# Where an odd chunk's stored factors are loaded: behind the even chunk's last tables, or at the odd chunk's turn

## The chip, the cores and the metric

The kernel runs on one core of a Trainium2 chip. The metric is the device time of one execution in microseconds; a comparison uses the median of several runs. The core has five engines that matter here, each with an instruction order of its own: TensorE (PE, matrix products), VectorE (DVE, elementwise work), ScalarE (ACT, exponentials, sines), GpSimd (POOL, here only an issuer of DMAs) and SyncE (SP, the main issuer of DMAs). An instruction at the head of an engine's order that waits for something holds up all behind it on that engine.

## The reference

Two independent computations on a sequence of 2048 with 576 channels stand side by side in the output. The first is a long convolution whose kernel K comes from a diagonal state space:

```python
P = jnp.exp(logdA[:, :, None] * l[None, None, :])
K = jnp.einsum("dn,dnl,dn->dl", Cc, P, dB).real
...
Kf = rfft2(K padded to 2L)
Uf = rfft2(u padded to 2L)
y = irfft2(Uf * Kf)[..., :L] + u * Dskip
```

The second is multi-query attention with 32 heads of 18 channels that share one key and one value head:

```python
q = (x @ wq).reshape(B, S, H, Dh)
k = x @ wk
v = x @ wv
p = softmax(einsum("bhqd,bkd->bhqk", q, k) * Dh ** -0.5)
o = einsum("bhqk,bkd->bhqd", p, v).reshape(B, S, H * Dh) @ wo
```

Everything is in float32.

## The kernel before

**Attention is the frame.** It runs over four query chunks of 512 rows, eight groups of four heads, sixteen blocks of 128 keys and two pairs of heads: 1024 score tiles, two to a step, so 512 steps. Each round of three tiles issues the scores on PE (L520), the exponentials on ACT (L531) and, some tiles later, the products with the values (L829). Beside this PE has filler work: the query projections (`q`), the output projections (`op`) and the whole convolution.

**The convolution runs in 12 chunks of 48 channels**, each in two halves that are generators:

- `front(k)` makes the kernel K of chunk k. `factors(k)` prepares three tiles of factors, `f`, `r` and `m` (128 x 1248 each, 624 KB), and the small `w`. Two half chunks follow, each with `tables(k, s)` on DVE, which multiplies the factors out into `tab`, and `kgen(k, s, ksb)` on PE, which contracts the tables into a PSUM bank that DVE copies to `ksb`. At the end `ksb` goes through DRAM (`kd`, L1234) into another layout (`kt`, L1236).
- `back(k)` transforms the input (`us`, from the matmuls hu and lu) and the kernel (`ks`, from hk and lk), multiplies the spectra (`pt`, `acc`) and transforms back (`iy`).

**Even and odd chunks differ in `factors`.** The factors need exponentials and sines from ACT, which interrupt the softmax and change ACT's table. So the even chunk k computes them for k and for k + 1 together, with the second set in one tile `two`, and stores `two` in DRAM (`parked`, L1146, shown as `park<-two`). The odd chunk k + 1 loads `f`, `r`, `m` and `w` from there (L1106) and begins with `r * m` and `f * m`. `f`, `r`, `m` and `w` have one buffer each, shared by all chunks, as do `sum` (which shares the buffer of `m`) and `tab`.

**The order of the engines.** PE, ACT, DVE and POOL run in the order in which the program issues their instructions; SP is not named there, so the framework may set the order of its DMAs by what is ready:

```python
with tc.manual_schedule(engines={mybir.EngineType.PE, mybir.EngineType.Activation, mybir.EngineType.DVE, mybir.EngineType.Pool}):
```

The order of the four is made by a planner while the program is built. A `Clock` carries the modelled times of PE (`t`), DVE (`v`) and ACT (`a`). The generators yield a kind, a time from which they are ready, and whether they hold the one PSUM bank for fillers: "v" is DVE work, "p" PE work, "w" waits, "b" waits for a good place for the block of sines. `Stream.go` lets a stream advance when its time has come and, for PE work, when there is credit. `Conv.turn` starts the next turn, `back(k)` beside `front(k + 1)`, only when both halves of the turn before have ended. In `factors`, the odd chunk yields "v" with the time `K.t + 7.0` behind its loads, so that the planner doesn't order `r * m` sooner than 7 us after them.

The constants at the top tune the planner: how far DVE is ordered ahead of PE (AHEAD), how much credit fillers get and keep (LEAST, CAP, DEBT, MOST), how large a gap must be (GAP, GAP_NEW), when a product is put off (DEFER), when the projections are ahead or late (LEAD, SLOPE, LEFT, URGENT), and so on.

Of the kernel before, what the change touches and what calls it, by code (L numbers as in the profile page):

```python
# [9 lines left out]
F32 = mybir.dt.float32  # L10
# [7 lines left out]
P = 128  # L18
# [19 lines left out]
NP = 8  # L38


RATE = 6.983
PACE = 1.7672
AHEAD = 0.4952
TOTAL = 604.4861
LAST = 813.2825
DEFER = 0.378
NAUG = 5
LEFT = 1.1655
CAP = 1.5491
DEBT = 0.6604  # L50
GROUP = 0.1377
HOLD = 0.3071
LEAD = 1.8204
MOST = 0.4269
LEAST = 0.3048
NEAR = 1.3779
SLOPE = 0.851
SOON = 1.3672
URGENT = 8.8421
BACK = 2  # L60
HELD = 0
GAP = 0.2663
GAP_NEW = 0.3191

LATE = {1: [0], 3: [1], 5: [2], 6: [3]}

ND = 48
NCK = D // ND
NSB = 2
TB = ND // 4 // NSB  # L70
NE = 4 * ND
NF = 26
# [5 lines left out]
class Clock:  # L78
# [13 lines left out]
    def near(self):  # L92

        return NEAR if self.t + SOON > min(self.due, self.last) else 0.0

# [58 lines left out]
class Stream:  # L154
# [3 lines left out]

    def __init__(self, gen, clock, ahead=AHEAD):
        self.gen, self.k, self.ahead = gen, clock, ahead  # L160
# [44 lines left out]
class Attention:  # L205
# [294 lines left out]
    def fetch(self, group):  # L500

        while self.next < min(64, 2 * group + NAUG) and 2 * self.next + 2 <= self.queried:
            c, pr = divmod(self.next, 16)
            t = self.aug[self.next].bitcast(F32)
            qd, sd = self.qd[c]
            for j in range(2):
                h = 2 * pr + j
                self.nc.sync.dma_start(t[64 * j:64 * j + 54, :], qd[:, h * DH:h * DH + DH, :])
                self.nc.sync.dma_start(t[64 * j + 54:64 * j + 55, :], sd[h:h + 1, :])
            self.ready.add(self.next)  # L510
            self.next += 1
# [226 lines left out]
    def late(self):  # L738

        s = self.step  # L740
        if self.due < 128 and self.due - s < 2 * self.q_left + 14:
            return True
        return (84, 168, 252, 282)[s // 128] - self.units > LEFT * (128 * (s // 128) + (120, 120, 120, 116)[s // 128] - s)

# [17 lines left out]
    def main(self, conv, flag):  # L762
# [22 lines left out]
        def fill(then, wait=True):  # L785
# [3 lines left out]
            while more:  # L789
# [3 lines left out]
                late = self.late()  # L793
                ahead = self.units - LEAD * self.step
                for st in (prep, side, conv) if urgent else (prep, conv, side):
                    if st is side and side.kind == "p" and not (urgent or side.holds) and conv.lags(self.step):
                        continue
                    spare = credit - LEAST
                    if st is side and not (urgent or late or side.holds):
                        spare -= SLOPE * max(ahead, 0.0)  # L800
                    elif st is side and side.holds:
                        spare += HOLD
                    wait = then - K.t - (GAP_NEW if st is side and not urgent and not side.holds else GAP)
# [13 lines left out]
            state["filled"] += K.t - t  # L817
            state["credit"] = max(state["credit"] - (K.t - t), -DEBT)

        def product(h):  # L820
# [11 lines left out]
            state["credit"] -= 0.44  # L832
            self.k.last = K.t + GROUP if kb >= 14 else 1e9
            if f == 0:
# [9 lines left out]
        for r in range(0, len(pairs), NS):  # L844
# [31 lines left out]

            state["credit"] = min(state["credit"] + NS / 2 * (0.88 + min(max((TOTAL - state["filled"]) / max(LAST - s, 20), 0.45), MOST)), CAP + 0.88)

# [4 lines left out]
            while behind < target:  # L883
                fill(free() - 0.44 * (target - behind), False)

                if behind >= target - 2 and K.t + 0.44 > free() + DEFER:
                    break
# [110 lines left out]
class Conv:  # L998
# [57 lines left out]
    def arguments(self, k, w, f, r, m):  # L1056
# [32 lines left out]
        if k > 1:  # L1089
            self.load(k + 2)  # L1090

    def factors(self, k):

        nc, V, p1, K = self.nc, self.V, self.pf, self.k
        tt = V.tensor_tensor
        mu, ad, sb = ALU.mult, ALU.add, ALU.subtract
        shp = [P, ND, NF]
        ch = lambda t, n: t.unsqueeze(2).broadcast_to([P, ND, n])
        w = p1.tile([P, 3, ND], F32, tag="w", name=f"w{k}")
        f = p1.tile(shp, F32, tag="f", name=f"f{k}")  # L1100
        r = p1.tile(shp, F32, tag="r", name=f"r{k}")
        m = p1.tile(shp, F32, tag="sum", name=f"m{k}")
        if k % 2:
            n = ND * NF
            for j, t in enumerate((f, r, m, w)):
                nc.sync.dma_start(t, self.parked[:, j * n:min((j + 1) * n, 3 * n + 3 * ND)].rearrange("p (c n) -> p c n", n=t.shape[2]))  # L1106
            yield "v", K.t + 7.0, False
        else:
            two = p1.tile([P, 3 * ND * NF + 3 * ND], F32, tag="tab", name=f"two{k}")
            part = lambda j, n: two[:, j * ND * NF:j * ND * NF + n * ND].rearrange("p (c n) -> p c n", n=NF if n == NF else ND)  # L1110
            f2, r2, m2, w2 = part(0, NF), part(1, NF), part(2, NF), part(3, 3)
            def sines(cos, sin):
                nc.scalar.activation(sin, sin, AF.Sin, scale=TWO_PI)
                nc.scalar.activation(cos, cos, AF.Sin, scale=-TWO_PI, bias=self.hp)
            one, two_ = self.arguments(k, w, f, r, m), self.arguments(k + 1, w2, f2, r2, m2)
            if k == 0:
                take = lambda g, n: [next(g, None) for _ in range(n)]
                take(one, 2)
                take(two_, 1)
                take(one, 1)  # L1120
                take(two_, 1)
                yield "v", 0.0, False
                take(one, 9)
                sines(r, f)
                yield "v", 0.0, False
                take(two_, 3)
                yield "v", 0.0, False
                take(two_, 9)
                sines(r2, f2)
                nc.scalar.activation(self.one, self.one, AF.Exp)  # L1130
                yield "v", 0.0, False
                for j in (2, 3):
                    self.load(j)
            else:
                yield from one
                yield "v", 0.0, False
                yield from two_
                yield "v", K.v + 0.3, False
                nc.scalar.activation(m, m, AF.Exp)
                nc.scalar.activation(m2, m2, AF.Exp)  # L1140
                K.act(2.5)
                yield "b", K.v + 0.3, False
                sines(r, f)
                sines(r2, f2)
            self.parked = self.dr.tile([P, 3 * ND * NF + 3 * ND], F32, tag="park", name=f"park{k}")
            nc.sync.dma_start(self.parked, two)  # L1146
            yield "v", K.act(7.7 if k > 0 else 0.0) + 0.3, False
        tt(r, r, m, op=mu)
        yield "v", 0.0, False
        tt(f, f, m, op=mu)  # L1150
        yield "v", 0.0, False

        c8 = lambda t: t[:, :, 0:8]
        t1 = p1.tile([P, ND, 8], F32, tag="tmp", name=f"t1_{k}")
        t2 = p1.tile([P, ND, 8], F32, tag="dif", name=f"t2_{k}")
        tt(t2, c8(r), ch(w[:, 1, :], 8), op=mu)
        tt(t1, c8(f), ch(w[:, 1, :], 8), op=mu)
        yield "v", 0.0, False
        tt(c8(r), c8(r), ch(w[:, 0, :], 8), op=mu)
        tt(c8(f), c8(f), ch(w[:, 0, :], 8), op=mu)  # L1160
        yield "v", 0.0, False
        tt(c8(r), c8(r), t1, op=sb)
        tt(c8(f), c8(f), t2, op=ad)
        sm = p1.tile(shp, F32, tag="sum", name=f"sum{k}")
        df = p1.tile([P, ND, 10], F32, tag="dif", name=f"dif{k}")
        yield "v", 0.0, False
        tt(df, f[:, :, 16:], r[:, :, 16:], op=sb)
        yield "v", 0.0, False
        tt(sm, r, f, op=ad)
        yield "v", 0.0, False  # L1170
        self.fac = r, f, sm, df
# [50 lines left out]
    def front(self, k):  # L1222

        nc = self.nc
        yield from self.factors(k)
        ksb = self.pf.tile([P, 4, NSB, 16, TB], F32, tag="ksb", name=f"ksb{k}")
        for s in range(NSB):
            yield from self.tables(k, s)
            yield from self.kgen(k, s, ksb)
        while self.kt is not None:  # L1230
            yield "w", 0.0, False
        kt = self.p1.tile([P, 4, NSB, 16, TB], F32, tag="kt", name=f"kt{k}")
        kd = self.dr.tile([P, 4, NSB * 16 * TB], F32, tag="kd", name=f"kd{k}")
        nc.sync.dma_start(kd, ksb.rearrange("p h s c d -> p h (s c d)"))  # L1234
        for h in range(4):
            nc.sync.dma_start(kt[32 * h:32 * h + 32].rearrange("p g s c d -> p g (s c d)"), kd[:, h].rearrange("(g p) x -> p g x", p=32))  # L1236
        self.kt, self.kt_ready = kt, self.k.t + 9.0
# [151 lines left out]
    def go(self, step, credit, lock):  # L1389
        self.turn()  # L1390
        lag = step * RATE - self.work
        if lag < -20.0:
            return False
        ahead = AHEAD + min(max(lag, 0.0) / 20.0, 1.0)
        for st in self.streams:
# [16 lines left out]
    def lags(self, step):  # L1412
        return self.work < step * PACE and any(st.live and st.kind == "p" for st in self.streams)

# [120 lines left out]
```

## Time and profile before

| | |
|---|---|
| median of 3 runs | 1183.37 us (1183.21 to 1183.97) |
| the profiled execution, its own time | 1182.26 us |
| its span, first to last instruction | 1180.1 us |
| mean clock granted to TensorE | 0.994 of full speed |
| bytes moved by DMA | 132.06 MB, on average 112 GB/s |
| softmax exponentials on ACT (L531) | 992 of 1032 ns, 941.3 us |
| products with the values on PE (L829) | 529.7 us |
| scores on PE (L520) | 349.5 us |

Times in the profile are microseconds from the start of the span unless marked ns. A row of a timeline has the start, the duration, the engine, the line, the operation with its output and inputs by name, the shape, the count, and in brackets the idle time before it with what ended that. SPq rows are DMAs as SP issues them: their duration is that of the issue, not of the transfer. A row of a table of groups ends with busy time, mean ns of one, the idle time before the group and what ended it. In a row of the waits stand who waited, for whom, the total in us, how often, and the longest. Rows of the chain of work that ended last have a start, a duration and what worked. Matmul durations overlap on PE, so its busy time is that of the engine and not a sum of durations.

### The profile page before, as it was taken

Reading aid. Unit: us, or ns where it says so; the run is one execution under the profiler, and the core shown is the slowest. Engines: PE = TensorE matmul, PEld = TensorE weight load, DVE = VectorE, ACT = ScalarE, POOL = GpSimd, SP = SyncE. Lnnn points to the kernel's source line nnn. Section 1 sums busy time; section 2 is a strip of 40 time slices with the busy share of each in tenths; the row PEclk is TensorE's granted clock in tenths of the full one; section 3 lists DMA queues with packets and bytes.
Section 4 is the critical chain, followed back from the end, with each engine's and each line's share of the span. In section 5 each row is a group of like instructions: output and inputs, shape, how many; then the busy total and the mean of one; then the engine's idle time right before and its main releaser. Section 6 shows DMA issues by size and latency. Waiting matters only on the chain.

```text
span 1180.1 us, 41335 instructions
## 1 busy us (share of the span) xinstructions
PE 1132.4 (96%) x17962; PEld 601.1 (51%) x17962; DVE 959.8 (81%) x1703; ACT 1038.0 (88%) x1092; POOL 95.0 (8%) x151
## 2 busy tenths in 40 slices
PE   7999999899999999999989999988999999999997
PEld 2555555455555455555545555544544545555553
DVE  7858979886997965996988698679799797799575
ACT  5899889889989988888998988888999998999993
POOL 2000201101110000011110000001000000000000
PEclk9999999999999999999999999999999999999999
DMA  8542443425333414224353421333422431431222
GB/s 303 168 141 79 129 143 92 148 94 196 89 116 91 140 53 144 72 75 159 86 186 111 149 53 46 106 98 117 143 70 66 131 123 63 157 87 38 84 63 71
DMA packets 55549, 132.06 MB, mean 112 GB/s; under 512 B 7612, under 2 KB 17436, under 8 KB 54083
## 3 DMA queue, kind: packets, MB, share of 16 engines
q1 hardware_dynamic: 43571, 96.03, 23.4%
q0 software_dynamic: 11504, 33.11, 11.1%
q8 instruction: 143, 2.34, 0.8%
q14 instruction: 43, 0.35, 0.1%
q10 hardware_dynamic: 288, 0.22, 0.1%
HBM read 61.57 MB, written 48.45 MB: 93 GB/s over the span
## 4 chain that ended last, share of the span: by engine, by line
PE 66%; DVE 25%; DMA 3%; ACT 3%; issue 2%; ACTq 0%; SPq 0%; DVEq 0%
PE ops L829 27%; PE s L520 19%; PE op L202 5%; PE q L202 4%; DVE acc L128 3%; DVE tab L128 3%; DVE ks L128 3%; PE kg L1215 3%; PE iy L202 3%; DVE pt L128 2%; ACT P L531 2%; DVE two L128 1%; PE lu L202 1%; PE lk L202 1%; PE hu L202 1%
## 5 line engine op out<-in xcount | busy, mean ns | idle before, releaser
L531 ACT ACTIVATE P<-s 128x1024 f32<-128x1024 f32 x992 | 941.3, 1032 | 105.6 <-PE s L520 97.0
L829 PE MATMUL ops<-P,v_sb 128*32 128x256 f32 x8192 | 529.7, 382 | 1.8 <-DVE o L132 1.5
L520 PE MATMUL s<-aug,kaug 55*128 55x512 f32 x2048 | 349.5, 437 | 9.4 <-ACT P L531 7.6
L829 PEld LDWEIGHTS ops<-P,v_sb 128*32 128x32 f32 x8192 | 248.1, 110 | 179.1 <-issue 43.9
L520 PEld LDWEIGHTS s<-aug,kaug 55*128 55x128 f32 x2048 | 166.7, 184 | 203.4 <-ACT P L531 109.1
L202 PE MATMUL op<-wo_sb,oT 126*32 126x288 f32 (+1 forms) x1152 | 85.1, 412 | 7.5 <-DVE ob L132 7.4
L202 PE MATMUL q<-x,wq_sb 128*32 128x256 f32 x1200 | 79.6, 392 | 4.2 <-DVE ql L128 2.3
L132 DVE COPY ksb<-kg 128x192 f32<-128x192 f32 x48 | 17.5, 364 | 65.9 <-PE kg L1215 65.9
L128 DVE TENSOR_TENSOR tab<-tab,tt 128x576 f32<-128x576 f32 (+1 forms) x72 | 59.2, 822 | 1.7
L128 DVE TENSOR_TENSOR tab<-sum,r 128x576 f32<-128x576 f32 (+1 forms) x72 | 58.8, 816 | 0.0
L128 DVE TENSOR_TENSOR tt<-f,sum 128x576 f32<-128x576 f32 (+1 forms) x72 | 58.7, 816 | 0.0
L128 DVE TENSOR_TENSOR tab<-r,dif 128x576 f32<-128x576 f32 (+1 forms) x72 | 58.7, 816 | 0.0
L128 DVE TENSOR_TENSOR tab<-tab 128x576 f32<-128x576 f32 (+1 forms) x72 | 58.7, 816 | 0.0
L202 PEld LDWEIGHTS q<-x,wq_sb 128*32 128x32 f32 x1200 | 36.3, 112 | 37.9 <-issue 12.2
L128 DVE TENSOR_TENSOR acc<-acc,pt 128x864 f32<-128x864 f32 (+2 forms) x72 | 54.3, 754 | 1.6
L202 PEld LDWEIGHTS op<-wo_sb,oT 126*32 126x32 f32 (+1 forms) x1152 | 32.2, 110 | 45.2 <-DVE ob L132 11.3
L128 DVE TENSOR_TENSOR pt<-us,ks 128x864 f32<-128x864 f32 (+2 forms) x72 | 54.1, 752 | 0.8
L1286 POOL DMA_DIRECT2D us<-us x12 | 6.7, 561 | 486.1 <-PE hk L202 188.9
L1215 PEld LDWEIGHTS kg<-tab 128*32 128x32 f32 x2304 | 36.1, 110 | 15.0 <-issue 6.7
L1215 PE MATMUL kg<-tab 128*32 128x64 f32 x2304 | 41.7, 220 | 1.3 <-DVE tab L128 0.9
L128 DVE TENSOR_TENSOR scu<-lu,scu 128x384 f32<-128x384 f32 x48 | 24.5, 551 | 20.5 <-PE lu L202 20.4
L128 DVE TENSOR_TENSOR u<-u,iy 128x384 f32<-128x384 f32 x24 | 13.3, 553 | 32.5 <-PE iy L202 32.5
(169 smaller groups left out, 1045.8 us busy)
## 6 DMA issues: line engine op xcount, KB each, us to landing
aug<-qd SPq DMA_DIRECT2D x124, 108.0 KB
park<-two SPq DMA_DIRECT2D x6, 1944.0 KB
us<-us POOLq DMA_DIRECT2D x24, 384.0 KB, 3.9
od<-o SPq DMA_DIRECT2D x31, 256.0 KB
qd<-qh POOLq DMA_DIRECT2D x30, 256.0 KB, 3.9
u<-u SPq DMA_DIRECT2D x12, 480.0 KB
kd<-ksb SPq DMA_DIRECT2D x12, 384.0 KB
kt<-kd SPq DMA_DIRECT2D x48, 96.0 KB
```

The source lines that it names most:

```text
L128: return self.v.tensor_tensor(out, a, b, **k)
L132: return self.v.tensor_copy(out, src)
L202: nc.tensor.matmul(ps[j:e], w[:, j:e], x, start=start, stop=stop, tile_position=(0, j))
L520: nc.tensor.matmul(ps[:, j, :], self.kaug[r, kb * P:(kb + 1) * P], t[r, :], start=True, stop=True)
L531: nc.scalar.activation(pt, ps, AF.Exp, scale=SCALE)
L829: nc.tensor.matmul(o_ps[32 * j:32 * j + 32, cs], self.v[:, kb, :], pts[2 * n + j // 2][:, j % 2, cs], start=(kb + f == 0), stop=(kb + f == ...
L1215: nc.tensor.matmul(ps[32 * g:32 * g + 32, d, :], t[:, :32], t[:, 32:], start=(j == 0), stop=(j == 1), tile_position=(0, 32 * g))
L1286: nc.gpsimd.dma_start(us[:, 0:4, :], us[:, 4:8, :])
```

## The change

The four tiles are allocated in a helper `four(k)`, for even and odd chunks alike. The four loads move from `factors(k)` of the odd chunk into `fetch(k + 1)`, which the even chunk's `front` calls between its last `tables` and its last `kgen`. The time from which the odd chunk's first product may be ordered is taken there too, as the planner's PE time plus 7.0. Nineteen of the planner's constants get other values.

```diff
-RATE = 6.983
-PACE = 1.7672
-AHEAD = 0.4952
-TOTAL = 604.4861
-LAST = 813.2825
-DEFER = 0.378
+RATE = 8.2131
+PACE = 1.8426
+AHEAD = 0.4667
+TOTAL = 612.9427
+LAST = 829.8085
+DEFER = 0.3504
 NAUG = 5
-LEFT = 1.1655
-CAP = 1.5491
-DEBT = 0.6604
-GROUP = 0.1377
-HOLD = 0.3071
-LEAD = 1.8204
+LEFT = 1.0879
+CAP = 1.6403
+DEBT = 0.9025
+GROUP = 0.1017
+HOLD = 0.3715
+LEAD = 1.7798
 MOST = 0.4269
-LEAST = 0.3048
-NEAR = 1.3779
-SLOPE = 0.851
-SOON = 1.3672
-URGENT = 8.8421
+LEAST = 0.2848
+NEAR = 1.2753
+SLOPE = 0.9384
+SOON = 1.5253
+URGENT = 8.9887
 BACK = 2
 HELD = 0
-GAP = 0.2663
-GAP_NEW = 0.3191
+GAP = 0.293
+GAP_NEW = 0.3092
...
+    def four(self, k):
+
+        p1, shp = self.pf, [P, ND, NF]
+        w = p1.tile([P, 3, ND], F32, tag="w", name=f"w{k}")
+        f = p1.tile(shp, F32, tag="f", name=f"f{k}")
+        r = p1.tile(shp, F32, tag="r", name=f"r{k}")
+        return f, r, p1.tile(shp, F32, tag="sum", name=f"m{k}"), w
+
+    def fetch(self, k):
+
+        n = ND * NF
+        self.fetched, self.fetched_at = self.four(k), self.k.t + 7.0
+        for j, t in enumerate(self.fetched):
+            self.nc.sync.dma_start(t, self.parked[:, j * n:min((j + 1) * n, 3 * n + 3 * ND)].rearrange("p (c n) -> p c n", n=t.shape[2]))
...
     def factors(self, k):
...
-        w = p1.tile([P, 3, ND], F32, tag="w", name=f"w{k}")
-        f = p1.tile(shp, F32, tag="f", name=f"f{k}")
-        r = p1.tile(shp, F32, tag="r", name=f"r{k}")
-        m = p1.tile(shp, F32, tag="sum", name=f"m{k}")
         if k % 2:
-            n = ND * NF
-            for j, t in enumerate((f, r, m, w)):
-                nc.sync.dma_start(t, self.parked[:, j * n:min((j + 1) * n, 3 * n + 3 * ND)].rearrange("p (c n) -> p c n", n=t.shape[2]))
-            yield "v", K.t + 7.0, False
+            f, r, m, w = self.fetched
+            yield "v", self.fetched_at, False
         else:
+            f, r, m, w = self.four(k)
...
             yield from self.tables(k, s)
+            if s == NSB - 1 and k % 2 == 0:
+                self.fetch(k + 1)
             yield from self.kgen(k, s, ksb)
```

## The prediction

> **What bounds the kernel now.** I first read the cores and the busy times.
>
> ```profile
> core 0: 1180.1 us, clock 0.994
> PE 1132.4 (96%) x17962; PEld 601.1 (51%) x17962; DVE 959.8 (81%) x1703; ACT 1038.0 (88%) x1092; POOL 95.0 (8%) x151
> ```
>
> TensorE (PE) is busy 96% of the span, so an edit that adds and removes no matmul can only move PE's idle time: 1180.1 - 1132.4 = 47.7 us in all. VectorE (DVE) has 1180.1 - 959.8 = 220.3 us idle. Next I read, for three of the six odd chunks, SP's order in time around the loads from `park`, and beside it DVE's.
>
> ```profile
> 74.75 0.33 SPq L1106 DMA_DIRECT2D r<-park  x1
> 84.61 0.32 SPq L1234 DMA_DIRECT2D kd<-ksb  x1
> ...
> 268.51 0.33 SPq L1106 DMA_DIRECT2D f<-park  x1
> 269.44 0.42 SPq L1106 DMA_DIRECT2D m<-park  x1
> 274.46 0.32 SPq L1234 DMA_DIRECT2D kd<-ksb  x1
> ...
> 459.57 0.35 SPq L1106 DMA_DIRECT2D f<-park  x1
> 460.07 0.34 SPq L1106 DMA_DIRECT2D r<-park  x1
> 462.05 0.32 SPq L1234 DMA_DIRECT2D kd<-ksb  x1
> 462.82 0.32 SPq L540 DMA_DIRECT2D od<-o  x1
> 463.19 0.50 SPq L1106 DMA_DIRECT2D m<-park  x1
> ...
> 838.50 0.32 SPq L1106 DMA_DIRECT2D r<-park  x1
> 839.53 0.43 SPq L1106 DMA_DIRECT2D m<-park  x1
> ```
>
> ```profile
> 269.19 0.76 DVE L128 TENSOR_TENSOR tab<-tab,tt 128x576 f32<-128x576 f32 x1
> 274.06 0.37 DVE L132 COPY ksb<-kg 128x192 f32<-128x192 f32 x1 [2.63 <-PE kg L1215]
> 282.03 1.45 DVE L128 TENSOR_TENSOR r<-r,m 128x1248 f32<-128x1248 f32 x1
> ...
> 458.12 0.76 DVE L128 TENSOR_TENSOR tab<-tab,tt 128x576 f32<-128x576 f32 x1
> 461.67 0.36 DVE L132 COPY ksb<-kg 128x192 f32<-128x192 f32 x1 [1.35 <-PE kg L1215]
> 471.93 1.46 DVE L128 TENSOR_TENSOR r<-r,m 128x1248 f32<-128x1248 f32 x1 [2.72 <-DMA m<-park]
> 474.67 0.55 DVE L132 COPY scu<-hu 128x384 f32<-128x384 f32 x1
> ...
> 839.84 0.76 DVE L128 TENSOR_TENSOR tab<-tab,tt 128x576 f32<-128x576 f32 x1
> 843.95 0.36 DVE L132 COPY ksb<-kg 128x192 f32<-128x192 f32 x1 [1.17 <-PE kg L1215]
> 849.61 1.45 DVE L128 TENSOR_TENSOR r<-r,m 128x1248 f32<-128x1248 f32 x1
> ```
>
> This says something that the diff does not. In the old text the loads are written behind `kd<-ksb` of the even chunk. On the chip they already stand ahead of it: chunk 1 issues r at 74.75 and kd at 84.61, chunk 3 issues f and m at 268.51 and 269.44 and kd at 274.46. SP isn't among the engines of `manual_schedule`; its order is the framework's, and it has pulled the loads forward to where their buffers come free, which is the even chunk's last tables (269.19, 458.12 and 839.84 are the last table instructions). The one exception in these rows is chunk 5, whose m goes behind kd and od. The chain that ended last and the waits show what that costs:
>
> ```profile
> 463.19 8.64 DMA m<-park
> ```
>
> ```profile
> DVE r L128 <- DMA m<-park: 2.7, 1, 2.7
> ```
>
> One wait in the whole run, 2.7 us of DVE, and it is on the chain. Behind it in DVE's order stands the copy `scu<-hu` (474.67), which empties the one fill bank, and PE waits for that bank:
>
> ```profile
> 475.28 0.86 PE L202 MATMUL lu<-u,dft_sb 128*32 128x192 f32 x16 [1.07 <-DVE scu L132]
> ```
>
> ```profile
> 470.00:480.00 10.00, 8.06 (x119) 4.61 (x123) 8.07 (x13) 7.82 (x10) 0.00 (x0) 1.00 0.32 98
> 200.00:220.00 20.00, 15.59 (x230) 8.03 (x226) 17.26 (x27) 17.29 (x18) 3.81 (x6) 0.91 0.54 189
> 400.00:410.00 10.00, 8.19 (x126) 3.93 (x128) 8.87 (x14) 9.94 (x10) 0.86 (x1) 1.00 0.60 196
> 590.00:615.00 25.00, 20.80 (x316) 11.35 (x308) 20.58 (x40) 23.27 (x24) 4.83 (x8) 1.00 0.54 189
> 780.00:800.00 20.00, 14.67 (x216) 6.90 (x212) 14.56 (x24) 15.02 (x15) 3.21 (x6) 0.91 0.43 152
> 950.00:970.00 20.00, 17.69 (x252) 8.56 (x254) 19.54 (x29) 19.10 (x19) 1.72 (x2) 1.00 0.39 103
> ```
>
> Of these stretches (length, then PE, PE's weight loads, DVE, ACT, POOL busy, then clock, DMA share, GB/s), the first is chunk 5: PE is idle 10.00 - 8.06 = 1.94 us. The other five are the even chunks' turns, where ScalarE leaves the softmax for the exponentials and sines of the factors: 4.41 + 1.81 + 4.20 + 5.33 + 2.31 = 18.1 us of PE's idle time, nearly ten times chunk 5's.
>
> **The change part by part.** No instruction is added or removed: the same four DMAs per odd chunk, the same arithmetic.
>
> *SP's order.* The loads are now written ahead of the even chunk's `kgen` and kd, so where both are ready they should go first. At chunks 3 and 9 they stand right at the last tables already, so nothing moves. At chunk 5, m goes ahead of kd and od, from 463.19 to about 460.4 (behind r at 460.07 and its 0.34 us), and no longer behind their bytes. If the data are then in time, DVE loses no 2.7 us and PE's 1.94 us go: **-1.9 us**, bounds -2.7 (the whole stall) and 0 (the same bank is late for another reason). What moves back is kd at chunk 5, by SP's half microsecond and m's transfer; `kt` waits for it, and the key transform that reads kt comes only after the input's transform, which had just begun at 474.67. That costs nothing.
>
> *The planner's ready time.* The order of DVE and PE is written out by a planner, and it lets the odd chunk's first product `r<-r,m` go 7.0 us after the load was emitted. The emission moves from behind the last `ksb` copy to behind the last table, in these rows from 274.06 to 269.19, 461.67 to 458.12, 843.95 to 839.84: 4.9, 3.5 and 4.1 us, mean 4.2. So in each of six odd turns DVE's first product can be ordered about 4 us earlier, 25 us in all, out of a lull (DVE has only the scu copies between 461.67 and 471.93). What is that worth at the end? Nothing at the place itself, where PE was full but at chunk 5. It is worth something where PE waits for DVE further on:
>
> ```profile
> L202 PE MATMUL op<-wo_sb,oT 126*32 126x288 f32 (+1 forms) x1152 | 85.1, 412 | 7.5 <-DVE ob L132 7.4
> L202 PE MATMUL q<-x,wq_sb 128*32 128x256 f32 x1200 | 79.6, 392 | 4.2 <-DVE ql L128 2.3 <-DVE un L140 1.7
> L202 PE MATMUL up<-aw,all 128*32 128x8 f32 (+2 forms) x288 | 5.7, 176 | 6.5 <-DVE aw L136 6.5
> ```
>
> 7.4 + 4.0 + 6.5 = 17.9 us of PE stand behind DVE's queue. Giving DVE 25 us of its 220.3 idle back at a better place is 11% of its slack; I take the same share of the 17.9: **-2.0 us**. Bounds 0 (the waits are elsewhere in the turn and untouched) and -17.9.
>
> *New stalls on the data.* The data do not arrive earlier, except at chunk 5, but the product may stand earlier. The old 7.0 us put `r<-r,m` 282.03 - 274.06 = 8.0, 10.3 - 2.7 = 7.5 and 849.61 - 843.95 = 5.7 us behind the emission point; on the new point that is about 276, 465 and 847. When do the data land? For chunk 9 the transfer rate shows it:
>
> ```profile
> 843.00:844.00 1.00, 1.00 (x54) 0.88 (x48) 0.05 (x1) 0.73 (x1) 0.00 (x0) 1.00 1.03 379
> 844.00:845.00 1.00, 1.00 (x14) 0.50 (x16) 0.30 (x1) 0.59 (x1) 0.00 (x0) 1.00 0.62 255
> ```
>
> The engines run full to 844 and ebb by 845, some 6 us after 838.50, so about 845 against 847: no stall. At chunk 5, 459.57 + 6 is 465.6 at the earliest, and at the latest 471.9 less kd's and od's 1.6 us (384 and 256 KB at some 400 GB/s), so 470.3, against 465: a stall of 0.6 to 5 us; a DVE stall there costs PE 1.94 / 2.72 = 0.7 of itself. I take 1.4 us on DVE, the low part, since m was the only one pushed back, and none elsewhere: **+1.0 us**, bounds 0 and 9.7 (the other five boundaries stall as chunk 5 did, 5 x 1.94).
>
> The Trainium skill, in "DMA: Bandwidth & Descriptors", section Bandwidth, puts the ceiling at 435 GB/s; three loads of 624 KB would then need an estimated 4.4 us and the latency, and the sum would hold no new stall (-3.9). The rate in chunk 9's row agrees with the ceiling, but chunk 5's landing, 8.64 us after its issue, is what I keep.
>
> *The retuned constants.* TOTAL and LAST do nothing: they enter as min(max(x, 0.45), MOST) with MOST 0.4269, which is always MOST. RATE does next to nothing: it sets a lag that is cut off at 20 us, and with at most 959.8 / 512 = 1.9 us of DVE work per step the lag, at 6.98 or 8.21 per step, is past that from step 4. The rest (GAP, CAP, LEAST, DEFER, AHEAD, LEAD, SLOPE, LEFT and so on) shift which filler goes into which gap. The first thing that such a shift moves is what is at hand when a sine block comes. The five blocks show the scatter: mean 3.6 us, standard deviation 1.5, so a fresh draw of five is worth 1.5 x sqrt(5) = 3.3 us either way. Value **0**, bounds -3.3 and +3.3.
>
> **Sum**: -1.9 - 2.0 + 1.0 + 0 = -2.9 us. The profiled execution took 1182.26 us (span 1180.1 and 2.2 around it), 1.1 below the median of the runs, 1183.37. It becomes 1179.4, and the median **1180.5**.
>
> **The rivals.** *It doesn't do what it says.* Five loads of six stand there already, and chunk 5's stall goes on with other causes, or half of it: 0 to -1.9 us, 1181.5 to 1183.4. For it: the rows of chunks 1, 3 and 9, and that PE is full at their boundaries. Against: the ready time moves in any case, and the constants.
>
> *The data come too late (slower).* Place: the first product of the odd chunks. Price: 1.94 us of PE each, as chunk 5 shows. It decides as soon as `r<-r,m` is ordered less than some 6 us (chunk 9) to 12 us (chunk 5, from 459.57 to 471.9) behind the first load. With 5 more boundaries, 1183.4 + 9.7 = 1193; with half of them 1188. For it: the 7.0 us now start 4 us sooner against the same landing, and 465 stands against 465.6 to 470. Against: chunk 9 has 2 us to spare.
>
> *The sine blocks are drawn worse (slower).* The forecast plus 3.3 us is 1183.8; what makes it more is the clock. In the blocks at 200 and 780 the granted clock is 0.91, a loss of 20 x 0.09 = 1.8 us each, and at 400, 590 and 950 it is 1.00. With the other three at 0.91 too: 1180.5 + 3.3 + 3 x 1.8 = 1189; with one, 1185.6. The Trainium skill, "TensorE: Matmul & The Clock Gate", Part 1, says that PE falls to half rate after an idle window of about 3.4 us, and needs as long to recover; the trace agrees on the size (1.8 us is half of 3.6), though the 590 block idles 4.20 us in pieces with its clock whole. The same draw can go the other way: 3.3 us less is 1177.2.
>
> **How the numbers follow.** A run of this kernel can be told from no change beyond about 0.2%, 2.4 us: faster is below 1181.0, slower above 1185.7. Forecast (with the better draw of blocks) 0.46; it doesn't do what it says, 0.22; data too late 0.15; worse blocks 0.17. The forecast's own range is 1177 to 1181; the whole range reaches from 1173, a better draw and twice the gain behind DVE, to 1191, between half and all of the late boundaries. Faster 0.46, same 0.22, slower 0.32.
>
> **What would show it.** Right: on SP, m of chunk 5 ahead of its kd; no wait of DVE for `park`; `r<-r,m` some 7 to 8 us behind the last table in place of 9.8 to 13.8; less than 17.9 us in the three waits. Wrong: several waits for `park` of over a microsecond, each with an idle PE behind it; or sine blocks with over 18.1 us of idle PE together or with a clock of 0.91 in three or more. If PE is busy as long as before and its idle time is moved to where the fillers have run out, at the end, the gain is gone too.

## The result, and the profile after

| | before | after |
|---|---|---|
| median, 11 runs each | 1183.37 us | 1186.25 us |
| ratio to before, with its 95% interval | | 1.0027 (1.0015 to 1.004) |
| its eleven runs | 1181.22 to 1185.75 | 1182.52 to 1189.2 |

The change makes the kernel slower by 0.27%, where 0.24% faster was forecast. It is inside the stated range and on the other side of no change. The first profile of the changed kernel is of the fastest of its eleven runs (1182.52 us, span 1180.3); I show a second one, of a usual run (1188.34 us, span 1186.2), which the experiments below brought under the name after_again. Its 12 runs gave a median of 1187.12 us and a ratio of 1.0021 (1.0008 to 1.0034) to the kernel before on the same chip. Here and below the ratios are not quotients of the medians: a difference taken from the one can differ from the other by 1 to 2 us. PE's busy time, from the page of that second profile, is 2.8 us more than before, and its idle time 51.0 us in place of 47.7.

```profile
span 1186.2 us, 41322 instructions
## 1 busy us (share of the span) xinstructions
PE 1135.2 (96%) x17962; PEld 601.8 (51%) x17962; DVE 961.3 (81%) x1702; ACT 1039.0 (88%) x1092; POOL 93.8 (8%) x151
```

The waits of the same profile (who, for whom, total us, times, longest) have the line that was to vanish, and it has grown from one wait of 2.7 us to four:

```profile
DVE r L128 <- DMA m<-park: 6.3, 4, 4.1
```

DVE's order in time at the four odd chunks where it waits, 3, 5, 7 and 9:

```profile
279.52 0.37 DVE L132 COPY ksb<-kg 128x192 f32<-128x192 f32 x1 [2.64 <-PE kg L1225]
284.02 1.46 DVE L128 TENSOR_TENSOR r<-r,m 128x1248 f32<-128x1248 f32 x1 [4.13 <-DMA m<-park]
285.40 0.68 DVE L132 COPY o<-ops 128x512 f32<-128x512 f32 x1
...
473.00 1.46 DVE L128 TENSOR_TENSOR r<-r,m 128x1248 f32<-128x1248 f32 x1 [0.42 <-DMA m<-park]
...
670.94 1.46 DVE L128 TENSOR_TENSOR r<-r,m 128x1248 f32<-128x1248 f32 x1 [1.54 <-DMA m<-park]
...
851.53 1.46 DVE L128 TENSOR_TENSOR r<-r,m 128x1248 f32<-128x1248 f32 x1 [0.16 <-DMA m<-park]
```

At chunk 3 the product stands right behind the last `ksb` copy, not some 8 us behind it as before, and it waits 4.13 us. (In the same row of the kernel before, in the prediction, nothing is waited for.) Behind it in DVE's order is `o<-ops`, the copy that frees the bank of the products with the values. PE's order in time shows who waits for that:

```profile
280.68 0.50 PE L520 MATMUL s<-aug,kaug 55*128 55x512 f32 x1
281.95 0.86 PE L520 MATMUL s<-aug,kaug 55*128 55x512 f32 x5 [0.78 <-issue]
282.74 0.86 PE L202 MATMUL hu<-u,dft_sb 128*32 128x192 f32 x16
286.14 2.79 PE L829 MATMUL ops<-P,v_sb 128*32 128x256 f32 x24 [2.54 <-DVE o L132]
```

And this is the same place microsecond by microsecond (PE, weight loads, DVE, ACT, POOL busy, then the granted clock, DMA share, GB/s):

```profile
280.00:281.00 1.00, 1.00 (x17) 0.36 (x10) 0.00 (x0) 1.00 (x2) 0.00 (x0) 1.00 1.02 414
281.00:282.00 1.00, 0.23 (x3) 0.05 (x2) 0.00 (x0) 0.16 (x1) 0.00 (x0) 1.00 0.74 298
...
283.00:284.00 1.00, 0.59 (x16) 0.19 (x8) 0.00 (x0) 1.00 (x2) 0.00 (x0) 1.00 0.27 97
284.00:285.00 1.00, 0.00 (x0) 0.00 (x0) 0.98 (x1) 1.00 (x2) 0.00 (x0) 0.57 0.20 78
285.00:286.00 1.00, 0.00 (x0) 0.00 (x0) 1.00 (x2) 0.30 (x1) 0.00 (x0) 0.50 0.91 366
286.00:287.00 1.00, 0.86 (x10) 0.41 (x14) 1.00 (x3) 0.00 (x0) 0.00 (x0) 0.50 0.30 114
...
290.00:291.00 1.00, 1.00 (x12) 0.40 (x12) 0.00 (x0) 1.00 (x2) 0.00 (x0) 0.51 0.33 103
291.00:292.00 1.00, 1.00 (x24) 0.60 (x20) 0.40 (x1) 1.00 (x2) 0.00 (x0) 1.00 0.77 198
```

PE is idle 0.77 + 0.41 + 1.00 + 1.00 + 0.14 = 3.3 us here, in two pieces. The second, 2.5 us, is the wait for DVE's copy `o`. The first, 0.8 us, stands before the scores and not behind DVE; the profile names no releaser for it. What fits is the loads of the scores' queries (`aug`), which go out right behind the four loads (275.44) while the DMA engines are full to 281 (share 1.02); that isn't shown. The clock falls to half within 284 to 285 (a mean of 0.57, so at about 284.1) and is back at 291. While PE is idle a lower clock costs nothing; from 286.14 to 291 PE is busy at half clock, which loses 4.8 x 0.5 = 2.4 us (the 24 products take 2.79 us; in small_loads, at full clock, 1.48). The 4.1 us wait on DVE is thus followed by 2.5 + 2.4 = 4.9 us lost on PE, and with the scores' wait it is 5.7 us. SP's order shows what stands ahead of the data:

```profile
270.84 0.36 SPq L236 DMA_DIRECT2D x<-xT  x1
273.74 0.32 SPq L1105 DMA_DIRECT2D f<-park  x1
274.11 0.48 SPq L1105 DMA_DIRECT2D r<-park  x1
274.64 0.71 SPq L1105 DMA_DIRECT2D m<-park  x1
275.44 0.72 SPq L508 DMA_DIRECT2D aug<-qd  x1
```

The 1280 KB of the next query chunk's `x` go out 2.9 us ahead, and the product starts 9.4 us after the issue of m. At chunks 5, 7 and 9, with no `x` ahead, that is 8.6, 7.4 and 6.3 us, so `x` can explain a part of the lateness (no run takes it away). The other part is the product's place: without its wait it would start 5.2 us after the issue of m here, and 8.2, 5.9 and 6.2 us after it there. The kernel before has the same neighbour at the same place, 3 us ahead of f:

```profile
265.46 0.34 SPq L236 DMA_DIRECT2D x<-xT  x1
```

There the product came at 282.03, and nobody saw the late data.

### The profile page after: what moved, and what is told of

It is laid out like the page before. It is cut to its first block, busy times and chain, and to the rows that moved or that the text cites. A ratio compares the mean times of both kernels' runs of the same rounds, so it can differ in the third digit from the quotient of the medians.

```text
span 1180.3 us, 41322 instructions
## 1 busy us (share of the span) xinstructions
PE 1131.5 (96%) x17962; PEld 600.2 (51%) x17962; DVE 960.9 (81%) x1702; ACT 1039.0 (88%) x1092; POOL 93.7 (8%) x151
## 4 chain that ended last, share of the span: by engine, by line
PE 62%; DVE 25%; DMA 5%; ACT 4%; issue 4%; POOL 0%; SPq 0%; ACTq 0%; DVEq 0%; POOLq 0%
PE ops L829 25%; PE s L520 18%; DVE tab L128 5%; PE op L202 4%; ACT P L531 3%; PE q L202 3%; DVE acc L128 3%; PE iy L202 3%; PE kg L1225 3%; DMA m<-park 2%; DVE ks L128 2%; DVE pt L128 1%; DVE tt L128 1%; PE lk L202 1%; PE lu L202 1%
## 5 line engine op out<-in xcount | busy, mean ns | idle before, releaser
L202 PE MATMUL q<-x,wq_sb 128*32 128x256 f32 x1200 | 77.2, 382 | 2.3 <-DVE ql L128 1.1
L202 PEld LDWEIGHTS op<-wo_sb,oT 126*32 126x32 f32 (+1 forms) x1144 | 32.7, 109 | 44.0 <-DVE ob L132 10.3
L202 PE MATMUL iy<-w,dft_sb 128*32 128x192 f32 x768 | 38.9, 337 | 4.9 <-DVE ql L128 4.2
```

Source lines behind the costliest of these rows:

```text
L202: nc.tensor.matmul(ps[j:e], w[:, j:e], x, start=start, stop=stop, tile_position=(0, j))
```

## The experiments

Two theories were put against each other. L, late data: DVE's first product is ordered some 4 us sooner, the loads don't land sooner, and DVE and PE wait. C, constants: the nineteen constants put fillers elsewhere, and that is the loss.

**The parts of the change by themselves.** First the new constants alone, in the kernel before:

```diff
-RATE = 6.983
+RATE = 8.2131
...
-GAP_NEW = 0.3191
+GAP_NEW = 0.3092
```

> The kernel before with the changed kernel's nineteen constants and nothing else: the loads are written at the odd chunk's turn, and the first product may be ordered 7.0 us after that. Theory L (late data: the product is ordered some 4 us sooner than before, DVE waits for the loads, PE behind it): the constants are not the cause, so 1181 to 1184 us, with at most one wait of DVE for park. Theory C (constants: they put other fillers around the sine blocks and the gaps): the whole loss is here, 1185.5 to 1188 us.

Measured: 1211.42 us, ratio 1.0256 (1.0235 to 1.0278). Neither theory had that. The tails of PE and ACT show most of it:

```profile
1185.34 2.79 PE L202 MATMUL iy<-w,dft_sb 128*32 128x192 f32 x32 [11.66 <-DVE w L128]
```

```profile
1170.99 1.02 ACT L531 ACTIVATE P<-s 128x1024 f32<-128x1024 f32 x1 [0.18 <-PE s L520]
```

The last exponential ends at 1172.0, but one of the convolution's last inverse transforms begins at 1185.34 behind 11.66 us of idle PE. Before, the two met:

```profile
1159.91 1.02 ACT L531 ACTIVATE P<-s 128x1024 f32<-128x1024 f32 x1 [0.87 <-PE s L520]
1160.20 1.48 PE L202 MATMUL iy<-w,dft_sb 128*32 128x192 f32 x32
```

The last exponential comes 11 us later than before, and the rest of the 28 us stands behind it, where the convolution runs on alone. There is one wait for `park` too, 6.7 us at chunk 3; how much of the 11 us it makes I did not separate.

Then the move alone, with the old constants:

```diff
+            if s == NSB - 1 and k % 2 == 0:
+                self.fetch(k + 1)
```

> The changed kernel with the constants of before. Theory L: three or more waits of DVE for park, 5 us or more together, and 1185 to 1189 us. Theory C: the move alone is worth nothing or a little, 1181 to 1184 us, whatever the waits for park are.

Measured: 1197.94 us, 1.0136 (1.0116 to 1.0155), with two waits for `park`, 4.4 us at chunk 3 and 3.9 at chunk 9. More than either theory said, with the waits that L foresaw in total but fewer of them.

Then only the early load, at the old constants, the ready time as before:

```diff
             f, r, m, w = self.fetched
-            yield "v", self.fetched_at, False
+            yield "v", K.t + 7.0, False
```

> The constants of before, the loads emitted behind the even chunk's last tables, but the first product's ready time taken at the odd chunk's turn, as before. PE, ACT, DVE and POOL have the order of the kernel before; only SP's order differs, at chunk 5, where m goes ahead of kd and od. Both theories: the 2.7 us wait of DVE at chunk 5 shrinks or goes, PE's 1.9 us idle there goes with it, 1181 to 1183.4 us. If it is 1183.4 or more with that wait gone, the wait at chunk 5 was worth nothing and my first term falls.

Measured: 1182.72 us, 0.9989 (0.9975 to 1.0003). SP issues m at 457.79, ahead of kd at 463.35; DVE has no wait for `park`; PE's idle time at 460 to 480 is 20.00 - 19.31 = 0.7 us, where it was 1.98 (the kernel before first, then this run):

```profile
460.00:480.00 20.00, 18.02 (x297) 9.88 (x301) 10.29 (x18) 16.24 (x19) 0.00 (x0) 1.00 0.58 189
460.00:480.00 20.00, 19.31 (x316) 10.18 (x314) 12.06 (x23) 16.45 (x19) 0.00 (x0) 1.00 0.48 168
```

So this is what the load's new place is worth by itself: 1.3 us here, not clear of the scatter in the time.

Last, the same edit in the changed kernel, so new constants and early load without the early ready time:

> The changed kernel, with its constants and its early loads, but with the first product's ready time taken at the odd chunk's turn as before. Theory L: the waits for park are gone and so is the loss, 1180 to 1183.5 us. Theory C: the loss stays, 1185.5 to 1188 us.

Measured: 1203.74 us, 1.0187 (1.0169 to 1.0206). The waits for `park` are gone, and the kernel is some 17 us slower than the changed one (19 by the ratios). L as I had put it falls here, and C too, since the loss is far beyond the change's. PE's tail explains it, and beside it that of the changed kernel's first profile:

```profile
1162.22 2.34 PE L829 MATMUL ops<-P,v_sb 128*32 128x256 f32 x40
1176.19 2.79 PE L202 MATMUL iy<-w,dft_sb 128*32 128x192 f32 x32 [11.62 <-DVE w L128]
1179.64 2.10 PE L202 MATMUL iy<-w,dft_sb 128*32 128x192 f32 x32 [0.66 <-DVE u L128]
```

```profile
1157.72 1.51 PE L202 MATMUL iy<-w,dft_sb 128*32 128x192 f32 x32
...
1160.96 2.77 PE L829 MATMUL ops<-P,v_sb 128*32 128x256 f32 x48
```

The attention ends at nearly the same time (1164.6 and 1163.7 for its last products), but without the early ready time the convolution ends 1179.64 - 1157.72 = 21.9 us later and runs on alone. With the new constants the early ready time of six odd turns brings the convolution about 22 us forward, near the 25 that I had reckoned; the 22 includes a tail in which PE waits 11.62 us, so that the two figures agree is in part luck. With the old constants it brings much less: the last inverse transform begins 3.2 us before the end of the attention's last products in e3_load_only (1164.84 and 1168.05) and 10.3 us before it in e2_move (1166.32 and 1176.62). The new constants alone cost 28 us, the move alone 14, and both together 3. The two parts can't be priced apart and added.

**The data waits by themselves.** For this the loads are made small, and the order of PE, ACT and DVE stays. The kernel leaves out 42 of the 48 channels of f, r and m, which keep the even chunk's values, so the convolution's output is another:

```diff
-        self.fetched, self.fetched_at = self.four(k), self.k.t + 7.0
+        old = self.fac[1], self.fac[0], self.fac[2]
+        self.fetched = *old, self.pf.tile([P, 3, ND], F32, tag="w", name=f"w{k}")
+        self.fetched_at = self.k.t + 7.0
...
+            c = 6 if j < 3 else 3
+            self.nc.sync.dma_start(t[:, 0:c, :], self.parked[:, j * n:j * n + c * t.shape[2]].rearrange("p (c n) -> p c n", n=t.shape[2]))
```

It ran with the new constants, with the old ones, at chunk 3 alone and at all but chunk 3, and the whole change once more beside them.

> The changed kernel once more, beside the next three on the same chip. Every theory: 1184 to 1188 us. Its profile so far was of its fastest run (1182.5 us, clock 0.996); a usual one should show the clock of 0.993 that most of its runs have, and so where the time goes that the fastest run doesn't lose: theory L says in waits of DVE for park and the cold TensorE behind them, theory C in the sine blocks.

> The changed kernel with only the first 6 of 48 channels of r, f and sum loaded, into the even chunk's own tiles, an eighth of the bytes; the other 42 channels of an odd chunk go on from the even chunk's values, so the convolution's output is not the reference's. PE, ACT and DVE keep the changed kernel's order exactly. Theory L: no wait of DVE for park is left, and the 3.5 us of PE's idle time and 1.7 us of lost clock at 270 to 290 go with it, and 1 to 2 us at chunks 7 and 9: 1179 to 1182.5 us. Theory C: the waits weren't the cause, 1185 to 1188 us.

> The same small loads in the kernel with the move and the constants of before (1198 us with whole loads, waits for park of 8.2 us together), the same part of the work left out. Theory L as the whole of that kernel's loss: back to 1183 to 1187 us. If the waits are only their own price there, some 8 us with PE's lost clock: 1189 to 1193 us, and the rest of its loss of 14 us is the order of the fillers, which these constants weren't made for. No effect: 1196 us or more.

> The changed kernel with the small loads (6 of 48 channels of r, f and sum, the rest from the even chunk's values) at chunk 3 alone; the five other odd chunks load all. Theory L with chunk 3 as the main place, because the 1280 KB of the second query chunk's x go out just ahead of its loads: the long wait of 4.1 to 4.3 us and the cold TensorE behind it go, the short waits stay, 1179 to 1183 us. If the short waits together cost as much: 1183 to 1185.5 us. Theory C: 1186 us or more.

> The reverse: whole loads at chunk 3, small loads at the five others (the same part left out there). Theory L with chunk 3 as the main place: the wait of about 4 us at chunk 3 stays, with 3 us or more of PE's idle time and a granted clock under 1 behind it, 1183 to 1186.5 us. If the short waits are the main place: 1179 to 1182 us.

| kernel | us | ratio to before (95%) | waits for `park`, us |
|---|---|---|---|
| after_again | 1187.12 | 1.0021 (1.0008 to 1.0034) | 6.3 in 4 |
| small_loads | 1177.65 | 0.9949 (0.9933 to 0.9965) | none |
| e2_move | 1197.94 | 1.0136 (1.0116 to 1.0155) | 8.2 in 2 |
| small_loads_old_constants | 1189.89 | 1.0053 (1.0038 to 1.0067) | none |
| small_chunk3 | 1180.42 | 0.9982 (0.9968 to 0.9996) | 2.3 in 3 |
| small_others | 1183.49 | 1.001 (0.9994 to 1.0025) | 3.5 in 1 |

Without the data waits the changed kernel is 9.5 us faster than with them (8.5 by the ratios), more than L expected, and 5.9 us faster than the kernel before. With the old constants the waits cost 8.0 us, and 6.3 us of loss stay that no wait for `park` explains. That leaves the planner's other order; where in it the 6.3 us lie I did not trace. L is right on the waits in both; that theory's large form, that they are all of e2_move's loss, missed.

Chunk 3 is the main place, as expected: its loads made small take the ratio from 1.0021 to 0.9982, some 4.6 us; the five others made small, to 1.001, some 1.3 us. The sum, 5.9, is short of 8.5 for all six (1.0021 to 0.9949); the intervals are 1.5 us either way each, so I don't read more into the gap. The two expectations on these held, 1180.42 in 1179 to 1183 and 1183.49 at the lower end of 1183 to 1186.5. The small loads also take 10 MB off the DMA engines and go out sooner (the third at 252.74 at chunk 3, and at 274.64 in after_again), and the scores no longer wait 0.8 us there, so a part of the 9.5 us could be that; the next experiment moves the same bytes.

One expectation on after_again missed. L had it that a usual run loses its time against the fastest one in the waits for `park`. The fastest run has the same four waits, 6.6 us together, and the same fall of the clock at chunk 3. Of the 5.9 us between the two spans 2.8 are lost before the first odd chunk: its product, which waits for nothing, starts at 83.24 in the fastest run and at 86.05 here, and from 30 to 40 us the granted clock is 1.00 there and 0.66 here.

**The order of the loads.** The first product needs r and m; f is needed by the second, 1.4 us later (2.4 us at chunk 3, where two copies stand between). In the changed kernel f and r or r and f go first and m last.

```diff
-        for j, t in enumerate(self.fetched):
+        for j in (1, 2, 0, 3):
+            t = self.fetched[j]
```

> The changed kernel with the loads in the order r, m, f, w in place of f, r, m, w: r and m, which the first product needs, no longer share the engines with f to the end. PE, ACT and DVE keep the changed kernel's order. Theory L: the waits for park shrink by about a third of the transfer each, 1.5 us at chunk 3, the shorter ones to nothing, and the time falls by 1 to 4 us, 1182 to 1185 us. Theory C: no effect, 1185 to 1188 us.

Measured: 1180.54 us, 0.9964 (0.9949 to 0.9979), better than expected, faster than both kernels, with nothing left out and the same bytes. One wait is left, at chunk 3:

```profile
DVE r L128 <- DMA m<-park: 2.6, 1, 2.6
```

PE at 280 to 300, first in after_again and then here:

```profile
280.00:300.00 20.00, 16.68 (x214) 8.39 (x210) 13.81 (x25) 13.21 (x15) 0.00 (x0) 0.83 0.35 125
```

```profile
280.00:300.00 20.00, 18.27 (x279) 9.98 (x276) 19.01 (x34) 17.20 (x19) 1.44 (x2) 1.00 0.33 114
```

The wait at chunk 3 is 1.5 us shorter and PE's idle time 1.6 us: 0.8 of it at the copy `o`, where PE now waits 1.7 us, and the rest at the scores, which no longer wait. The clock of 0.83 is now 1.00, worth the 2.4 us above. Together that is 4.0 of the 6.6 us between the two kernels; the other waits for `park`, which are gone too, are the likely rest. With 1.7 us of idle PE in one piece the clock doesn't fall here.

## Why the prediction was wrong

*SP's order and chunk 5: right.* m of chunk 5 stands ahead of kd, and alone this takes 1.98 to 0.7 us of idle time off PE (-1.9 predicted, -1.3 found in the trace of e3_load_only; in the time it is not clear of the scatter).

*The ready time: right in that the work comes forward, not in what it was to be worth.* The first product stands earlier (8.4 us behind the start of the last table at chunks 1 and 5, 6.4 at chunk 9, by the first profile, waits included), and with the new constants the convolution comes forward by 22 us. PE's three waits for DVE are 12.7 us in after_again, down from 17.9, but two others grew, `o` from 1.5 to 5.7 and those of `iy` from 1.1 to 3.9:

```profile
L829 PE MATMUL ops<-P,v_sb 128*32 128x256 f32 x8192 | 529.1, 382 | 7.4 <-DVE o L132 5.7 <-issue 1.4
L202 PE MATMUL op<-wo_sb,oT 126*32 126x288 f32 (+1 forms) x1144 | 83.0, 410 | 8.2 <-DVE ob L132 6.4 <-DVE oT L128 1.6
L202 PE MATMUL q<-x,wq_sb 128*32 128x256 f32 x1200 | 79.3, 390 | 2.4 <-DVE ql L128 1.4 <-DVE ob L132 0.6 <-DVE un L140 0.4
L202 PE MATMUL iy<-w,dft_sb 128*32 128x192 f32 x768 | 37.7, 329 | 4.0 <-DVE ql L128 3.1 <-DVE u L128 0.8
L202 PE MATMUL up<-aw,all 128*32 128x8 f32 (+2 forms) x288 | 5.9, 179 | 5.3 <-DVE aw L136 4.5 <-DVE scu L128 0.8
```

The five together are 22.3 us, where they were 20.5; without the data waits, in small_loads, they are 19.7, so 0.8 us is gained there and not 2.0. By small_loads the change without data waits is worth -5.9 us, where -1.9 - 2.0 + 0 = -3.9 was predicted. That the two are near each other is in part luck: the five sine blocks below have 2.4 us less idle time in small_loads than before, a term put at 0.

*New stalls on the data: the step that failed.* The prediction took +1.0 us, "the low part", at chunk 5 and "none elsewhere". The runs show 9.5 us with the loads made small, and 6.6 got back by the order of the loads alone. The mechanism was in the prediction as the rival "the data come too late", at 1188 for half the boundaries, which had 0.15, and the bound of 9.7 held; the term was mis-sized. Three things were wrong in it. The landing was read off the transfer rate of chunk 9, 6 us after the first load, and taken for all chunks but 5. Where DVE waits for the data, the product starts 7.4 us after the first load at chunk 9, 8.5 at chunk 7, 9.7 at chunk 5 and 10.3 at chunk 3. Chunk 3's landing was never looked up, though the load of x stood 3 us ahead of its loads. The wait falls on whatever stands behind the product, at chunk 3 not the filler's bank but the one copy that the products with the values need. And a price of 0.7 us of PE per microsecond of wait came from a stall that left the clock alone; at chunk 3 it is 4.9 / 4.1 = 1.2, because the clock adds 2.4 us to the 2.5 of idle time. The page "TensorE: Matmul & The Clock Gate" of the Trainium skill, Part 1, which the prediction used for the sine blocks alone, says half rate after about 3.4 us of idling. Chunk 3 doesn't bear out that size: the clock fell at about 284.1, when PE had been idle 0.77 us and then, after working, 0.6 us.

*The constants: 0 is neither shown nor refuted, and the bounds were wrong.* With the whole change the five sine blocks keep 17.9 us of idle time, by these windows, against 20.5 in the same windows before:

```profile
200.00:240.00 40.00, 36.76 (x566) 19.23 (x564) 34.91 (x65) 37.94 (x39) 6.32 (x10) 1.00 0.43 140
400.00:420.00 20.00, 18.10 (x256) 8.73 (x260) 17.80 (x29) 19.34 (x20) 2.41 (x3) 1.00 0.36 93
580.00:640.00 60.00, 52.27 (x774) 26.66 (x766) 49.69 (x94) 50.28 (x52) 12.35 (x21) 0.97 0.53 171
780.00:820.00 40.00, 37.48 (x552) 18.59 (x544) 39.27 (x66) 36.66 (x38) 3.98 (x6) 1.00 0.43 138
950.00:980.00 30.00, 27.46 (x384) 13.29 (x382) 27.35 (x44) 27.52 (x27) 1.72 (x2) 1.00 0.44 139
```

That is 2.6 us less, inside my 3.3 us, in the direction of a better draw. But the constants alone cost 28 us and the move with the old ones 6.3 us without any wait, so 3.3 is no bound for either part by itself. I had looked at what is at hand in a sine block; for the constants alone the larger lever is whether convolution and attention end together, which stood in the tail of before (1159.91 and 1160.20) and had no place in the sum.

*It doesn't do what it says: false.* The loads stood there already at five chunks of six, as said, but the ready time alone, with the new constants, moved the convolution's end by 22 us. The rival's own row was right, and its conclusion wrong.

Left open: how much of the 9.5 us comes from the 10 MB less and the loads' earlier place, what chunks 5, 7 and 9 cost each, what part `x` has in the late data at chunk 3, and what the scores wait for there; r_m_first, with all bytes, gets 6.6 of the 9.5.

## What to carry to other kernels

When a planner's ready time is moved forward, look up for each place when the data land, what goes out ahead of them on the same queue, and order the loads by which operand is needed first. A stall has to be priced by the operation queued behind it and by whether the granted clock falls behind it: here 2.5 us of idle PE cost about as much again at half clock, and 1.7 us cost nothing more. The planner's constants don't transfer from one structure to another: the same nineteen numbers cost 28 us in the old structure and, in the new one, stand in a kernel that is 5.9 us faster than before once its data waits are gone.

## What the hardware showed beyond that

The clock fell after idle time in pieces, and not after a fixed length of it. In after_again PE was idle 0.77 us at 281 to 282, busy through 282 to 283, and idle again from 283.6; the clock was at half from about 284.1, with 2.0 us of that idle time still to come. At the same place in the first profile it fell at 283.1, after pieces of 1.2 and 1.9 us, and in small_others at 284.9, after pieces of 0.5 and 2.1 us, when PE was already working again. In r_m_first one piece of 1.7 us left it whole. In the three traces where it fell it came back after PE had been busy again for 4.8, 3.0 and 4.0 us. The Trainium skill ("TensorE: Matmul & The Clock Gate", Part 1) gives about 3.4 us of sustained work for that, which lies among the three. In the changed kernel's runs the mean clock and the time go together: 0.996 at 1182.52 us, and 0.993 in all six of its eleven runs from 1186.25 us up.
